# A list scheduler that takes a PSUM bank as one place, and another order of the three groups of a down turn

## The chip, the core and the metric

The kernel runs as one program on one core of one Trainium2 chip. The metric is device time in microseconds (us). Below, PE is TensorE, PEld its weight loads, DVE VectorE, ACT ScalarE, POOL GpSimd and SP the engine whose queue issues the DMAs.

## What is computed

A Performer attention (4 batches, 8 heads, 576 positions), then a mixture of 8 experts over all 2304 tokens, weighted by a Sinkhorn-normalised gate, then one dense layer with a swish. All in fp32.

```python
x = attention(q, k, v, omega)              # [2304, 512]
P = np.exp(x @ w_gate - max)               # [2304, 8]
for _ in range(8):
    P /= P.sum(1, keepdims=True) + 1e-09
    P /= P.sum(0, keepdims=True) + 1e-09
    P *= N / E
for e in range(E):
    out += P[:, e:e + 1] * (np.maximum(x @ w1[e], 0.0) @ w2[e])
h = out @ w_in
g = h * (1.0 / (1.0 + np.exp(-1.702 * h)))
return g @ w_out
```

## The kernel before

The attention comes first, with expert 0 woven into it (`e0_visit`, products on lines 716 and 773). Experts 1 to 7 and the dense layer follow in 54 **visits**, numbered 0 to 53 here: 18 pairs of 256-wide slices of the hidden layer (14 of experts, `l` = 0; 4 of the dense layer, `l` = 1) by 3 blocks of 768 tokens. A visit multiplies by Strassen's scheme (seven products in place of eight) in fp32 that is split into a high and a low part, three matmuls to a product term:

- `up_fast` makes the hidden layer: for each of the pair's two slices `c`, seven products of 6 matmuls (line 1152, 128x384): 84 matmuls in a visit. Their sums and differences are taken by ACT, DVE and POOL in banks 0 to 4 and 7 and in SBUF, and give the operands `h`.
- `down` multiplies `h` by the second weights: seven products `n` = 0 to 6, each in two **turns** (`c` = 0, then `c` = 1), each turn three **groups** `t` = 0, 1, 2 of 3 matmuls (line 1294, 128x256): 126 matmuls. The order of turns is written out in `TURNS`: (0,0), (0,1), (3,0), (1,0), (1,1), (2,0), (2,1), (3,1), (4,0), (4,1), (5,0), (5,1), (6,0), (6,1); the last one stands behind the first product of the next visit.

A PSUM bank holds two results of 256 columns. `PLACES` says where a group accumulates: "C" (n = 0, 2, 4, 6) in bank 5 (both halves, t = 0 and 1) and the first half of bank 6 (t = 2); "E" (n = 3, 5) in bank 7 (both halves) and the second half of bank 6; "D" (n = 1) in banks 0, 2 and 1. **So bank 6 belongs to C and to E.** After its turn c = 1 every group is evicted: by ACT into the banks of D for n = 0 (line 1311), otherwise onto the accumulator in SBUF by DVE (line 1329 for experts, line 1322 for the dense layer). A write to a bank waits in the running kernel until every earlier read of that bank is over, whichever half was read.

That order is made by `Plan`, a list scheduler that runs while the kernel is built. `rec` adds an operation with its engine, an assumed duration and the keys that it reads and writes. Operations that are `main` (all products of visits) stay on PE in the order written. `Plan.run` walks a modelled clock: each engine takes, when it is free, the arrived operation with the earliest due time; the resulting order is then issued. An operation marked "VP" may go to DVE or POOL. Before the change a bank's two halves are two keys (`spread` turns a whole bank into both), and a DVE or ACT operation occupies its engine for its whole duration. The Sinkhorn iterations (`sinkhorn`, lines 849 to 870, one small PE matmul each on line 862) are planned in the same way, among expert 0's last visits and visit 0. `y_operands` (transposes on line 955, sums on line 972) rebuilds operands at the change from experts to dense layer, in visits 40 to 43; `double_piece` (lines 1082 to 1106) converts the dense layer's weights, a few DVE operations a visit, during the experts.

Of the kernel before, what the change touches and what calls it, by code (L numbers as in the profile page):

```python
# [14 lines left out]
ALU = mybir.AluOpType  # L15
# [9 lines left out]
class Plan:  # L25
# [9 lines left out]
    AHEAD = 3.0  # L35

# [56 lines left out]
    def run(self):  # L93
# [12 lines left out]
        while done < len(self.ops):  # L106
# [66 lines left out]
def tile_performer_sinkhorn_moe(  # L173
# [437 lines left out]
    def spread(keys):  # L611

        return [h for k in keys for h in ([k + (0,), k + (1,)] if k[0] == "b" and len(k) == 2 else [k])]

    def rec(eng, dur, fn, r=(), w=(), **kw):
# [3 lines left out]
        else:  # L619
            plan.add(eng, dur, fn, spread(r), spread(w), **kw)  # L620
# [7 lines left out]
    def ps_us(n):  # L628
        return 0.17 + 0.001 * n
# [195 lines left out]
    def sinkhorn():  # L825
# [22 lines left out]
        for _ in range(NITER):  # L848
            dve(lambda: V.tensor_reduce(out=r[:, :, 0], in_=pg, op=ALU.add, axis=AX.X), ["lg"], ["r"])
            dve(lambda: V.tensor_scalar(out=r, in0=r, scalar1=1e-9, scalar2=None, op0=ALU.add), ["r"], ["r"], 0.12)  # L850
            dve(lambda: V.reciprocal(out=rr, in_=r), ["r"], ["rr"], 0.2)
            dve(
                lambda: V.tensor_tensor(out=pg, in0=pg, in1=rr.to_broadcast([P, NTILE, E]), op=ALU.mult),
                ["lg", "rr"], ["lg"],
# [3 lines left out]
                ["lg"], ["cs"],  # L858
# [9 lines left out]
            dve(lambda: V.reciprocal(out=rc[:, 0, :], in_=ct), ["ct"], ["rc"], 0.15)  # L868
# [5 lines left out]
                ["lg", "rc"], ["lg"],  # L874
# [406 lines left out]
    def down(l, e, j, first, final):  # L1281

        touched = set()
        for n, c in TURNS[l]:
# [3 lines left out]
            for t in range(3):  # L1288
# [3 lines left out]
                def fn(e, i=i, u=u, t=t, c=c, a=a, slot=slot, start=start, half=half):  # L1292
                    for m, (x, y) in enumerate(((0, 0), (0, 1), (1, 0))):
                        nc.tensor.matmul(  # L1294
                            bank[i][:, u], T["h", c, a, x][:, t * P : (t + 1) * P], T["w2", c, y][:, slot],
                            start=start and half == 0 and c == 0 and m == 0, stop=c == 1 and m == 2,
                            skip_group_check=True,
                        )

                wr = [("b", i, half)]  # L1300
                if start and half == 0 and c == 0:
                    wr = [("b", i)]
                rec("PE", 3 * 0.118, fn, down_reads(c, a, slot), wr, main=True)
                if c == 0:
                    continue
                rd = [("b", i, half)]
                if n == 0:
# [3 lines left out]
                        lambda e, i=i, d=d, u=u: nc.scalar.copy(bank[d][:, 0:FC], bank[i][:, u]),  # L1311
                        [("b", i, half)], [("b", d)],
# [213 lines left out]
```

## Time and profile before

| | us |
|---|---|
| median of 3 runs (lowest, highest) | 2136.28 (2135.95, 2139.05) |
| the profiled execution's own time | 2134.32 |
| its span, first to last instruction | 2132.6 |

In the profile a row of PE is a run of equal matmuls, with its start, its length and the number of instructions; in square brackets stands the idle time before it and what ended that. Matmuls overlap: the distance from one start to the next is the pace, not the duration of one.

### The profile page before, as it was taken

What the parts mean: (1) busy time and instruction counts of PE and PEld (TensorE: products, weight loads), DVE (VectorE), ACT (ScalarE), POOL (GpSimd) and SP (SyncE); (2) the same over time, 40 slices, a digit from 0 to 9 for tenths busy, and PEclk for the clock granted to TensorE, in tenths of its full rate; (3) what the DMA queues carried; (4) which work ended last, traced back from release to release, by engine and by line L of the source; (5) the groups of instructions that cost most, each with busy time, mean ns of one, the idle gap of its engine ahead of it and who ended that gap; (6) DMA issues with size and microseconds to landing.
All of it is one profiled execution on the core that took longest, in us unless ns stands there. A gap on an engine that the chain in (4) does not pass through costs nothing.

```text
span 2132.6 us, 38364 instructions
## 1 busy us (share of the span) xinstructions
PE 2054.1 (96%) x13938; PEld 1977.8 (93%) x13938; DVE 1484.8 (70%) x2962; ACT 1050.4 (49%) x2444; POOL 1149.9 (54%) x1086
## 2 busy tenths in 40 slices
PE   9999998799999999999999999999999989999998
PEld 8999987799999999999999999999999979999998
DVE  7666559867667766777766776777666776667766
ACT  7655544355444443544444354444435466745644
POOL 3112239548465764747666574756647364737442
PEclk9999999999999999999999999999999999999999
DMA  8333238747556655746665675566456797645543
GB/s 165 85 80 90 70 98 300 248 175 276 193 205 239 245 192 216 261 179 222 253 224 187 227 259 191 208 256 222 184 207 227 240 294 252 235 152 212 221 175 128
DMA packets 255948, 431.46 MB, mean 202 GB/s; under 512 B 73744, under 2 KB 197136, under 8 KB 255760
## 3 DMA queue, kind: packets, MB, share of 16 engines
q1 hardware_dynamic: 255760, 429.02, 57.9%
q8 instruction: 110, 1.80, 0.3%
q14 instruction: 78, 0.64, 0.1%
HBM read 382.81 MB, written 46.14 MB: 201 GB/s over the span
## 4 chain that ended last, share of the span: by engine, by line
PE 79%; DVE 14%; ACT 2%; issue 2%; DMA 2%; POOL 1%; SPq 0%; DVEq 0%; ACTq 0%; POOLq 0%
PE bank L1152 34%; PE bank L1294 31%; DVE acc L1329 6%; PE ph L716 3%; PE py L773 3%; PE num L431 2%; DVE ring L639 1%; DMA sx<-stage 1%; PE kv L401 1%; DVE acc L1322 1%; DVE h L639 1%; PE pt L342 1%; DVE bank L1173 1%; PE pj L367 1%; PE pj L368 1%
## 5 line engine op out<-in xcount | busy, mean ns | idle before, releaser
L1294 PE MATMUL bank<-w,h 128*128 128x256 f32 x6804 | 892.8, 286 | 47.9 <-DVE acc L1329 28.4
L1294 PEld LDWEIGHTS bank<-w,h 128*128 128x128 f32 x6804 | 848.4, 191 | 86.4 <-DVE acc L1329 49.7
L1152 PE MATMUL bank<-xo,w 128*128 128x384 f32 x4536 | 821.5, 336 | 2.8 <-ACT ring L1162 1.9
L1152 PEld LDWEIGHTS bank<-xo,w 128*128 128x128 f32 x4536 | 783.7, 189 | 5.8 <-ACT ring L1162 4.0
L639 POOL TENSOR_TENSOR w<-raw,w 128x768 fp32r<-128x768 f32 (+1 forms) x216 | 327.5, 1524 | 313.4 <-ACT w L1058 302.6
L1329 DVE SCALAR_TENSOR_TENSOR acc<-bank,lg,acc 128x256 f32<-128x256 f32 x756 | 319.5, 478 | 200.8 <-PE bank L1294 200.0
L639 POOL TENSOR_TENSOR h<-ring,h 128x384 fp32r<-128x384 f32 x321 | 348.5, 1107 | 133.9 <-ACT h L1162 130.1
L1162 ACT ACTIVATE ring<-bank 128x384 f32<-128x384 f32 x432 | 210.2, 491 | 132.5 <-PE bank L1152 125.9
L1162 ACT ACTIVATE bank<-bank 128x384 f32<-128x384 f32 x108 | 51.4, 476 | 442.1 <-PE bank L1152 419.1
L1162 ACT ACTIVATE h<-ring 128x384 fp32r<-128x384 f32 x432 | 207.1, 527 | 87.4 <-DVE ring L1184 63.2
L639 POOL TENSOR_TENSOR raw<-raw 128x256 f32<-128x256 f32 x283 | 212.0, 774 | 47.0 <-DMA raw<-in_moe_w_dram 27.5
L1211 DVE SCALAR_TENSOR_TENSOR h<-bank,h 128x384 fp32r<-128x384 f32 x252 | 137.2, 552 | 120.5 <-ACT ring L1162 103.5
L1162 ACT ACTIVATE h<-bank 128x384 fp32r<-128x384 f32 x324 | 157.6, 492 | 62.8 <-DVE bank L1173 34.9
L1184 DVE SCALAR_TENSOR_TENSOR ring<-bank,ring 128x384 f32<-128x384 f32 x336 | 172.4, 548 | 20.6 <-PE bank L1152 20.0
L1058 ACT CAST w<-raw 128x768 fp32r<-128x768 f32 (+1 forms) x216 | 146.6, 691 | 81.0 <-POOL raw L639 65.2
L639 POOL TENSOR_TENSOR ring<-ring,ring 128x384 f32<-128x384 f32 (+1 forms) x97 | 103.4, 1066 | 142.9 <-ACT ring L1162 139.8
L695 POOL TENSOR_TENSOR egl<-raw,egh 128x512 fp32r<-128x512 f32 x32 | 41.9, 1327 | 187.4 <-ACT egh L692 168.9
L1173 DVE TENSOR_TENSOR bank<-bank,ring 128x384 f32<-128x384 f32 x216 | 120.9, 561 | 30.4 <-PE bank L1152 27.9
L639 DVE TENSOR_TENSOR h<-ring,h 128x384 fp32r<-128x384 f32 x111 | 112.0, 1024 | 22.4 <-ACT h L1162 21.9
L387 ACT ACTIVATE feat<-pj,nb 128x128 f32<-128x128 f32 x272 | 74.2, 387 | 67.2 <-DVE nb L383 64.9
L1322 DVE TENSOR_TENSOR acc<-bank,acc 128x256 f32<-128x256 f32 x180 | 65.7, 418 | 40.4 <-PE bank L1294 40.0
L1173 DVE TENSOR_TENSOR bank<-bank,sig 128x384 f32<-128x384 f32 x96 | 53.5, 561 | 50.1 <-ACT sig L1162 48.8
(231 smaller groups left out, 2084.2 us busy)
## 6 DMA issues: line engine op xcount, KB each, us to landing
xo<-sx SPq DMA_DIRECT2D x378, 768.0 KB, 7.1
raw<-in_moe_w_dram SPq DMA_DIRECT2D x288, 128.0 KB, 4.4
sx<-stage SPq DMA_DIRECT2D x126, 128.0 KB, 4.2
sx<-ring SPq DMA_DIRECT2D x48, 192.0 KB, 2.6
raw<-in_moe_w_dram SPq DMA_DIRECT2D x16, 512.0 KB, 4.1
stage<-in_moe_w_in_dram SPq DMA_DIRECT2D x16, 512.0 KB, 8.0
stage<-in_moe_w_out_dram SPq DMA_DIRECT2D x16, 512.0 KB, 6.7
k<-in_k_dram SPq DMA_DIRECT2D x16, 256.0 KB, 4.1
```

The costliest lines, as they stand in the source:

```text
L387: nc.scalar.activation(f[:, h, :], pvs[h // 4][:, h % 4, :], AF.Exp, bias=nb[:, h : h + 1])
L639: lambda e: e.tensor_tensor(out=out(), in0=a(), in1=b(), op=op),
L716: nc.tensor.matmul(o, ws[a], xs[b], start=m == 0, stop=m == n - 1, skip_group_check=True)
L1058: lambda e, a=a, b=b: nc.scalar.copy(T[w, c, 0][:, a:b], r[:, a:b]), raws, [(w, c, g, 0)],
L1152: nc.tensor.matmul(o(b), T["w1", c, a][:, slot, kk], T["xo"][x][:, y, kk], start=start and kk == 0 and n == 0, stop=kk == 1 and n == 2, sk ...
L1162: rec("ACT", act_us(Q), lambda e: nc.scalar.activation(out(), src(), f, **kw), r, w)
L1173: lambda e: e.tensor_tensor(out=out[0](), in0=a[0](), in1=b[0](), op=op), [a[1], b[1]], [out[1]],
L1184: lambda e: e.scalar_tensor_tensor(out=RT(out), in0=o(b), scalar=0.0, in1=RT(c), op0=ALU.max, op1=op),
L1211: lambda e: e.scalar_tensor_tensor(out=g(), in0=src[0](), scalar=0.0, in1=h().bitcast(F32), op0=ALU.max, op1=ALU.subtract),
L1294: nc.tensor.matmul(bank[i][:, u], T["h", c, a, x][:, t * P : (t + 1) * P], T["w2", c, y][:, slot], start=start and half == 0 and c == 0 an ...
L1322: lambda e, q=q, i=i, u=u: e.tensor_tensor(out=q, in0=bank[i][:, u], in1=q, op=ALU.add),
L1329: lambda e, q=q, i=i, u=u, g=g: e.scalar_tensor_tensor(out=q, in0=bank[i][:, u], scalar=g, in1=q, op0=ALU.mult, op1=ALU.add),
```

## The change

Four things are changed in the planner and the order it is given, and none in what is computed:

1. A bank is one key: `spread` is gone, and an eviction reads, a group writes `("b", i)`.
2. In a turn c = 1 the groups are taken in the order t = 2, 0, 1, and for n = 3 in the order 0, 2, 1; in turns c = 0 as before. The evictions of a turn are recorded behind its third group, in the same order.
3. An engine other than PE is free again 0.07 us before its operation's end (`LEAP`), and a PE operation that had to wait is planned 0.1 us longer (`RESTART`).
4. Assumed durations: a down group 0.36 in place of 0.354, an eviction on line 1329 0.05 longer, and the Sinkhorn steps.

```diff
+    LEAP = 0.07
+    RESTART = 0.1
...
-                o = None
+                o, rest = None, 0.0
...
                         if t - at["PE"] > 0.02:
+                            rest = self.RESTART
...
-                    d = o.dur[e] if isinstance(o.dur, dict) else o.dur
-                    o.end = at[e] = t + d
+                    d = (o.dur[e] if isinstance(o.dur, dict) else o.dur) + rest
+                    o.end = t + d
+                    at[e] = o.end if e in ("PE", "X") else o.end - self.LEAP
...
-            plan.add(eng, dur, fn, spread(r), spread(w), **kw)
+            plan.add(eng, dur, fn, r, w, **kw)
...
-            dve(lambda: V.tensor_scalar(out=r, in0=r, scalar1=1e-9, scalar2=None, op0=ALU.add), ["r"], ["r"], 0.12)
+            dve(lambda: V.tensor_scalar(out=r, in0=r, scalar1=1e-9, scalar2=None, op0=ALU.add), ["r"], ["r"], 0.3)
...
-            for t in range(3):
+            order = (0, 1, 2) if c == 0 else (0, 2, 1) if n == 3 else (2, 0, 1)
+            for t in order:
...
-                def fn(e, i=i, u=u, t=t, c=c, a=a, slot=slot, start=start, half=half):
+                def fn(e, i=i, u=u, t=t, c=c, a=a, slot=slot, s=start and half == 0 and c == 0):
...
-                wr = [("b", i, half)]
-                if start and half == 0 and c == 0:
-                    wr = [("b", i)]
-                rec("PE", 3 * 0.118, fn, down_reads(c, a, slot), wr, main=True)
-                if c == 0:
-                    continue
-                rd = [("b", i, half)]
+                rec("PE", 3 * 0.12, fn, down_reads(c, a, slot), [("b", i)], main=True)
+            if c == 0:
+                continue
+            for t in order:
+                i, half = PLACES[b][t]
+                u = slice(half * FC, (half + 1) * FC)
+                rd = [("b", i)]
...
-                        "DVE", ps_us(FC),
+                        "DVE", ps_us(FC) + 0.05,
```

The other planned Sinkhorn durations go to 0.27 and 0.2 (the reciprocals, from 0.2 and 0.15), 0.98 (the row scaling, from 0.3), 0.43 (the column sum, from 0.3) and 0.7 (the column scaling, from 0.3).

On PE, in the turn n = 4, c = 1 of an expert visit (`h14..` is its operand; `bank5`, `bank6` the banks), before:

```order
L1294 MATMUL bank5_3771<-w210_4561,h140_4571 128x256
L1294 MATMUL bank5_3771<-w211_4562,h140_4571 128x256
L1294 MATMUL bank5_3771<-w210_4561,h141_4572 128x256
L1294 MATMUL bank5_3771<-w210_4561,h140_4571 128x256
L1294 MATMUL bank5_3771<-w211_4562,h140_4571 128x256
L1294 MATMUL bank5_3771<-w210_4561,h141_4572 128x256
L1294 MATMUL bank6_3772<-w210_4561,h140_4571 128x256
L1294 MATMUL bank6_3772<-w211_4562,h140_4571 128x256
L1294 MATMUL bank6_3772<-w210_4561,h141_4572 128x256
```

and now:

```order
L1295 MATMUL bank6_3772<-w210_4560,h140_4570 128x256
L1295 MATMUL bank6_3772<-w211_4561,h140_4570 128x256
L1295 MATMUL bank6_3772<-w210_4560,h141_4571 128x256
L1295 MATMUL bank5_3771<-w210_4560,h140_4570 128x256
L1295 MATMUL bank5_3771<-w211_4561,h140_4570 128x256
L1295 MATMUL bank5_3771<-w210_4560,h141_4571 128x256
L1295 MATMUL bank5_3771<-w210_4560,h140_4570 128x256
L1295 MATMUL bank5_3771<-w211_4561,h140_4570 128x256
L1295 MATMUL bank5_3771<-w210_4560,h141_4571 128x256
```

The group in bank 6 has moved from third place to first.

On DVE, the evictions of one expert visit from n = 1 (banks 0, 1, 2) to n = 5, before:

```order
L1329 SCALAR_TENSOR_TENSOR acc0_126<-bank0_3766,lg_77,acc0_126 128x256
L1329 SCALAR_TENSOR_TENSOR acc0_126<-bank2_3768,lg_77,acc0_126 128x256
L1329 SCALAR_TENSOR_TENSOR acc0_126<-bank1_3767,lg_77,acc0_126 128x256
L639 TENSOR_TENSOR h141_4572<-ring9_3793,h140_4571 128x384
L1329 SCALAR_TENSOR_TENSOR acc0_126<-bank5_3771,lg_77,acc0_126 128x256 x2
L1329 SCALAR_TENSOR_TENSOR acc0_126<-bank6_3772,lg_77,acc0_126 128x256
L1329 SCALAR_TENSOR_TENSOR acc0_126<-bank7_3773,lg_77,acc0_126 128x256 x2
L1329 SCALAR_TENSOR_TENSOR acc0_126<-bank6_3772,lg_77,acc0_126 128x256
L1329 SCALAR_TENSOR_TENSOR acc0_126<-bank5_3771,lg_77,acc0_126 128x256 x2
L1329 SCALAR_TENSOR_TENSOR acc0_126<-bank6_3772,lg_77,acc0_126 128x256
```

and now:

```order
L639 TENSOR_TENSOR h121_4567<-ring11_3795,h120_4566 128x384
L1328 SCALAR_TENSOR_TENSOR acc0_126<-bank1_3767,lg_77,acc0_126 128x256
L1328 SCALAR_TENSOR_TENSOR acc0_126<-bank0_3766,lg_77,acc0_126 128x256
L1328 SCALAR_TENSOR_TENSOR acc0_126<-bank2_3768,lg_77,acc0_126 128x256
L1328 SCALAR_TENSOR_TENSOR acc0_126<-bank6_3772,lg_77,acc0_126 128x256
L1328 SCALAR_TENSOR_TENSOR acc0_126<-bank5_3771,lg_77,acc0_126 128x256 x2
L1328 SCALAR_TENSOR_TENSOR acc0_126<-bank6_3772,lg_77,acc0_126 128x256
L1328 SCALAR_TENSOR_TENSOR acc0_126<-bank7_3773,lg_77,acc0_126 128x256 x2
L1328 SCALAR_TENSOR_TENSOR acc0_126<-bank6_3772,lg_77,acc0_126 128x256
L1328 SCALAR_TENSOR_TENSOR acc0_126<-bank5_3771,lg_77,acc0_126 128x256 x2
```

Bank 6 is now evicted ahead of the pair in bank 5 or 7 of the same turn, where it stood behind it.

On PE in visit 0, the sixth of the eight Sinkhorn matmuls (line 862) among the up products, before:

```order
L1152 MATMUL bank3_3769<-xo0_3777,w111_4179 128x384
L1152 MATMUL bank3_3769<-xo0_3777,w110_4178 128x384
L862 MATMUL bank7_3773<-sm_153,ones_72 128x8
L1152 MATMUL bank0_3766<-xo4_3781,w100_4176 128x384
L1152 MATMUL bank0_3766<-xo4_3781,w101_4177 128x384
```

and now:

```order
L1152 MATMUL bank1_3767<-xo5_3782,w101_4181 128x384
L1152 MATMUL bank1_3767<-xo5_3782,w100_4180 128x384
L862 MATMUL bank7_3773<-sm_153,ones_72 128x8
L1152 MATMUL bank4_3770<-xo1_3778,w110_4182 128x384
L1152 MATMUL bank4_3770<-xo1_3778,w111_4183 128x384
```

It stands two products (12 matmuls) later. The seventh and the eighth stand where they stood, next to each other behind the tenth product: five products after the sixth before, three now.

## Rows read from the trace of the kernel before

**Rows 1.** The page's head and PE's busy share (us, share, instructions).
```profile
span 2132.6 us, 38364 instructions
...
PE 2054.1 (96%) x13938; PEld 1977.8 (93%) x13938; DVE 1484.8 (70%) x2962; ACT 1050.4 (49%) x2444; POOL 1149.9 (54%) x1086
```

**Rows 2.** The page's chain that ended last: share by engine, then by line.
```profile
PE 79%; DVE 14%; ACT 2%; issue 2%; DMA 2%; POOL 1%; SPq 0%; DVEq 0%; ACTq 0%; POOLq 0%
```

**Rows 3.** Busy time by stretch: visits 1 to 39, 40 to 42, 43 to 52.
```profile
core 0: us, PE busy (x) PEld busy (x) DVE busy (x) ACT busy (x) POOL busy (x), PEclk, DMA share, GB/s
441.02:1661.79 1220.77, 1193.09 (x8193) 1165.07 (x8192) 847.89 (x1684) 546.16 (x1209) 744.50 (x691) 1.00 0.60 219
1661.79:1779.93 118.14, 103.62 (x705) 99.97 (x703) 89.46 (x198) 71.38 (x180) 57.77 (x56) 0.96 0.91 284
1779.93:2095.58 315.65, 308.69 (x2102) 299.45 (x2101) 214.53 (x444) 179.65 (x416) 165.24 (x156) 1.00 0.56 204
```

**Rows 4.** Timeline of PE, one visit without waits at its start: pace of both products.
```profile
724.84 12.65 PE L1152 MATMUL bank<-xo,w 128*128 128x384 f32 x72
737.33 1.23 PE L1294 MATMUL bank<-w,h 128*128 128x256 f32 x9
738.39 1.21 PE L1152 MATMUL bank<-xo,w 128*128 128x384 f32 x6
```

**Rows 5.** Timeline of PE, the end of visit 19: three waits.
```profile
1029.00 3.61 PE L1294 MATMUL bank<-w,h 128*128 128x256 f32 x27 [0.28 <-DVE acc L1329]
1032.89 2.42 PE L1294 MATMUL bank<-w,h 128*128 128x256 f32 x18 [0.28 <-DVE acc L1329]
1035.60 0.62 PE L1294 MATMUL bank<-w,h 128*128 128x256 f32 x3 [0.28 <-DVE acc L1329]
...
1037.10 1.23 PE L1294 MATMUL bank<-w,h 128*128 128x256 f32 x9
1038.17 2.07 PE L1152 MATMUL bank<-xo,w 128*128 128x384 f32 x11
```

**Rows 6.** Timeline of PEld, the second of these waits.
```profile
1032.89 2.21 PEld L1294 LDWEIGHTS bank<-w,h 128*128 128x128 f32 x18 [0.49 <-DVE acc L1329]
```

**Rows 7.** Timeline of DVE, the same stretch: evictions in threes.
```profile
1031.57 1.27 DVE L1329 SCALAR_TENSOR_TENSOR acc<-bank,lg,acc 128x256 f32<-128x256 f32 x3 [1.43 <-PE bank L1294]
1034.27 1.27 DVE L1329 SCALAR_TENSOR_TENSOR acc<-bank,lg,acc 128x256 f32<-128x256 f32 x3 [1.43 <-PE bank L1294]
...
1038.02 1.27 DVE L1329 SCALAR_TENSOR_TENSOR acc<-bank,lg,acc 128x256 f32<-128x256 f32 x3 [1.42 <-PE bank L1294]
```

**Rows 8.** Who waited for whom, whole kernel (us, times, longest).
```profile
DVE acc L1329 <- PE bank L1294: 200.0, 188, 2.5
...
PEld bank L1294 <- DVE acc L1329: 49.7, 105, 0.8
...
PEld bank L1294 <- DVE acc L1322: 8.0, 25, 0.7
```

**Rows 9.** Waits of PE alone in visits 1 to 39.
```profile
PE bank L1294 <- DVE acc L1329: 27.0, 97, 0.5
PE bank L1152 <- ACT ring L1162: 0.6, 3, 0.2
```

**Rows 10.** Groups by shape, whole kernel (busy us, mean ns, idle before).
```profile
L1329 DVE SCALAR_TENSOR_TENSOR acc<-bank,lg,acc 128x256 f32<-128x256 f32 x756 | 319.5, 478 | 200.8 <-PE bank L1294 200.0
...
L639 DVE TENSOR_TENSOR h<-ring,h 128x384 fp32r<-128x384 f32 x111 | 112.0, 1024 | 22.4 <-ACT h L1162 21.9
...
L1322 DVE TENSOR_TENSOR acc<-bank,acc 128x256 f32<-128x256 f32 x180 | 65.7, 418 | 40.4 <-PE bank L1294 40.0
...
L1311 ACT COPY bank<-bank 128x256 f32<-128x256 f32 x162 | 53.7, 365 | 47.0 <-PE bank L1294 44.3 <-DVE ring L1184 2.0
```

**Rows 11.** Timeline of DVE around visit 19: two steps of `double_piece`.
```profile
1035.46 0.42 DVE L1082 TENSOR_SCALAR stage<-stage 128x512 uint32<-128x512 uint32 x1
1035.91 0.69 DVE L1086 SCALAR_TENSOR_TENSOR stage<-stage 128x512 uint32<-128x512 uint32 x1
```

**Rows 12.** Timeline of PE in visit 0: the seventh and eighth Sinkhorn matmuls (two instructions each).
```profile
403.68 5.45 PE L1152 MATMUL bank<-xo,w 128*128 128x384 f32 x30
413.71 0.60 PE L862 MATMUL bank<-sm,ones 128*128 128x8 f32 x2 [4.58 <-DVE sm L857]
418.14 0.60 PE L862 MATMUL bank<-sm,ones 128*128 128x8 f32 x2 [3.84 <-DVE sm L857]
419.60 5.34 PE L1152 MATMUL bank<-xo,w 128*128 128x384 f32 x18 [0.86 <-DVE bank L1173]
```

**Rows 13.** Timeline of DVE there: operations between the Sinkhorn steps.
```profile
407.50 0.41 DVE L639 TENSOR_TENSOR raw<-raw 128x256 f32<-128x256 f32 x1
...
411.85 1.48 DVE L639 TENSOR_TENSOR raw<-raw 128x256 f32<-128x256 f32 x1
```

**Rows 14.** Timeline of PE in visits 41 and 42: the longest waits.
```profile
1719.82 1.43 PE L1294 MATMUL bank<-w,h 128*128 128x256 f32 x9 [4.20 <-DVE stage L972]
...
1762.13 2.29 PE L1294 MATMUL bank<-w,h 128*128 128x256 f32 x9 [6.62 <-DVE stage L972]
```

More of the change, by code (lines that the diff above doesn't have):

```diff
@@ L609, in tile_performer_sinkhorn_moe @@
     live = [True]
-    def spread(keys):
-        return [h for k in keys for h in ([k + (0,), k + (1,)] if k[0] == "b" and len(k) == 2 else [k])]
     def rec(eng, dur, fn, r=(), w=(), **kw):
@@ L849, in sinkhorn @@
             dve(lambda: V.tensor_reduce(out=r[:, :, 0], in_=pg, op=ALU.add, axis=AX.X), ["lg"], ["r"])
-            dve(lambda: V.tensor_scalar(out=r, in0=r, scalar1=1e-9, scalar2=None, op0=ALU.add), ["r"], ["r"], 0.12)
-            dve(lambda: V.reciprocal(out=rr, in_=r), ["r"], ["rr"], 0.2)
+            dve(lambda: V.tensor_scalar(out=r, in0=r, scalar1=1e-9, scalar2=None, op0=ALU.add), ["r"], ["r"], 0.3)
+            dve(lambda: V.reciprocal(out=rr, in_=r), ["r"], ["rr"], 0.27)
             dve(
                 lambda: V.tensor_tensor(out=pg, in0=pg, in1=rr.to_broadcast([P, NTILE, E]), op=ALU.mult),
-                ["lg", "rr"], ["lg"],
+                ["lg", "rr"], ["lg"], 0.98,
             )
@@ L857, in sinkhorn @@
                 lambda: V.tensor_reduce(out=cs, in_=pg.rearrange("p t e -> p e t"), op=ALU.add, axis=AX.X),
-                ["lg"], ["cs"],
+                ["lg"], ["cs"], 0.43,
             )
@@ L867, in sinkhorn @@
             )
-            dve(lambda: V.reciprocal(out=rc[:, 0, :], in_=ct), ["ct"], ["rc"], 0.15)
+            dve(lambda: V.reciprocal(out=rc[:, 0, :], in_=ct), ["ct"], ["rc"], 0.2)
             dve(
@@ L873, in sinkhorn @@
                 ),
-                ["lg", "rc"], ["lg"],
+                ["lg", "rc"], ["lg"], 0.7,
             )
@@ L1295, in fn @@
                             bank[i][:, u], T["h", c, a, x][:, t * P : (t + 1) * P], T["w2", c, y][:, slot],
-                            start=start and half == 0 and c == 0 and m == 0, stop=c == 1 and m == 2,
-                            skip_group_check=True,
-                        )
-                wr = [("b", i, half)]
-                if start and half == 0 and c == 0:
-                    wr = [("b", i)]
-                rec("PE", 3 * 0.118, fn, down_reads(c, a, slot), wr, main=True)
-                if c == 0:
-                    continue
-                rd = [("b", i, half)]
+                            start=s and m == 0, stop=c == 1 and m == 2, skip_group_check=True,
+                        )
+                rec("PE", 3 * 0.12, fn, down_reads(c, a, slot), [("b", i)], main=True)
[5 more added lines that the diff above has]
+                rd = [("b", i)]
                 if n == 0:
@@ L1310, in down @@
                         "ACT", act_us(FC),
-                        lambda e, i=i, d=d, u=u: nc.scalar.copy(bank[d][:, 0:FC], bank[i][:, u]),
-                        [("b", i, half)], [("b", d)],
+                        lambda e, i=i, d=d, u=u: nc.scalar.copy(bank[d][:, 0:FC], bank[i][:, u]), rd, [("b", d)],
                     )
```

## The prediction

> **What bounds the kernel now.** I read the page's head first: PE is busy 96% of the span [rows 1], and the chain that ended last is PE for 79% and DVE for 14% [rows 2]. So PE sets the time, and the question is what PE waits for in its own stream. The stretches tell where the span lies: visits 1 to 39 take 1220.8 us, visits 40 to 42 take 118.1, visits 43 to 52 take 315.7 [rows 3]. Everything else (attention, expert 0, visit 0, the last visit) issues much the same order as before.
>
> What would visits 1 to 39 cost without a wait? The pace of an up matmul is (737.33 - 724.84)/72 = 0.1735 us, that of a down matmul (738.39 - 737.33)/9 = 0.118 [rows 4], or (1038.17 - 1037.10)/9 = 0.119 [rows 5]. A visit is then 84 x 0.1735 + 126 x 0.119 = 29.6 us and 39 of them 1153; 68 us are lost, 1.7 a visit. The waits name the loser: DVE's eviction on line 1329 ends 97 waits of PE in these visits, ACT 3 [rows 9].
>
> The timeline shows one such wait closely. Three times at the end of visit 19 PE stops for an eviction, with 18 matmuls between two stops [rows 5]. The profile shows 0.28 us idle, but that isn't the price: weights are held too, for 0.49 us [rows 6], and from one stopped matmul to the next 18 matmuls take 1035.60 - 1032.89 = 2.71 us in place of 2.16 or a little less. **A stop costs 0.55 us**, and 97 of them are 53 of the 68 us.
>
> Why it stops: 18 matmuls are two turns, so the stop is at the same place of each turn pair, the third group (bank 6). DVE evicts in threes, 0.395 us from start to start ((1.27 - 0.48)/2), and starts the first of them at 1031.57 [rows 7], so the third starts at 1032.36 and ends at 1032.84; PE goes on at 1032.89 [rows 5]. That third eviction was bank 6's, behind the pair of bank 5 or 7. PE fills bank 6 as the third group of a turn, wants it again as the third group of the next, two groups later, and gets there first. That it waits although the other half is meant shows that a bank is one place in the running kernel.
>
> **The change, part by part.**
>
> *Bank 6 first, and evicted first.* I set a turn c = 1 at time 0, matmuls 0.119 apart. How long an eviction starts behind the last matmul of its group I read at visit 20's start: the sixth of nine matmuls begins at 1037.10 + 5 x 0.119 = 1037.70 [rows 5], the first eviction at 1038.02 [rows 7]; so 0.32 us. Bank 6's group now begins its last matmul at 0.24, its eviction runs 0.56 to 1.04, and PE may write at 1.09.
> - n = 2 to n = 3: the next write of bank 6 is the 13th matmul, at 1.43, its weights 0.12 earlier. 0.2 us to spare.
> - n = 3 to n = 4 (n = 3 evicts bank 6 as soon as DVE is through with n = 2, at 2.07; done at 2.6): wanted at 2.9. 0.3 to spare.
> - n = 4 to n = 5 and n = 5 to n = 6: wanted as the 16th matmul, at 1.79, its weights at 1.67. 0.6 to spare.
>
> So the stops at bank 6 go. In the whole kernel PE's weights waited 105 times, 49.7 us, for line 1329 and 25 times, 8.0 us, for line 1322 [rows 8]; with the 0.06 by which a stop costs more than its 0.49, that is 57.7 + 130 x 0.06 = 65.5 us. About 1.5 of it is in visits 40 to 42, where other waits follow: **64 us** off. Of the 68 - 53 = 15 us that the stops don't explain, some are waits too short to show, next to the stops; I count a third, **5 us**. The ends are 0 and 15.
>
> *What is late next.* The pair of bank 5 or 7 is now evicted behind its second group, which is the turn's last. For n = 2: last matmul at 0.95, evictions at 1.27 and 1.67, the second over at 2.14, PE free to write at 2.19. The turn (4,0) wants bank 5 as the 19th matmul, at 2.14, its weights at 2.02. **PE comes 0.17 us too early**, in every visit. The trace of before doesn't hold this wait; its ends are 0 (if 0.32 is a little long) and a full stop, 0.55. I take 0.17, worked out from the spacing: 40 visits x 0.17 = 6.8. For n = 3, 4 and 5 the pair has a turn more and is through in time. In 8 expert visits the new DVE order has a step of `double_piece` (0.42 or 0.69 us [rows 11]) ahead of one of n = 2's or n = 3's or n = 4's bank evictions; I charge 0.3 each (ends 0 and 0.7): 2.4. In two visits an eviction of n = 1 has come between bank 6 and bank 5: 2 x 0.4 = 0.8. In the 11 visits of the dense layer an eviction of n = 1 often comes there too; its duration is 0.418 [rows 10], the stop then some 0.25: 2.8. Together **12.8 us** back on.
>
> The Trainium skill (VectorE: DVE Perf Modes, The DRAIN you can't avoid) says that the next operation doesn't start until the engine's pipe is empty, though one that isn't held may. By the first half the second eviction would end 0.08 later and 51 visits would lose 4 us more; the spacing of 0.395 against 0.48 [rows 7] speaks for the overlap.
>
> *Copies of n = 0.* They are taken by ACT behind the turn's third group, 0.36 us later than before for t = 0; 0.365 each [rows 10]. Bank 0 is wanted a turn later (1.07 us), bank 2 a group after it: copies over at 1.27 + 0.37 = 1.64 and 2.0, against 2.02 and 2.38. Covered while ACT is free; it waited 44 us for PE before these copies [rows 10]. Ends 0 and 3, I take **1.5 us** lost.
>
> *Sinkhorn.* PE idles 4.58 + 3.84 + 0.86 us around the last two matmuls of line 862 [rows 12]. They stand behind the same ten products now, so PE gains only if DVE ends sooner. On DVE the order up to the last Sinkhorn step has two operations of line 639 fewer, 0.4 to 1.5 us each [rows 13]; but the sixth matmul is 12 x 0.1735 = 2.1 us later in PE's stream, and work that lay between the seventh and eighth steps lies before the seventh. **1.5 us** off, ends 8 off and 5 on.
>
> *Operands of the dense layer.* Visits 41 and 42 wait 4.20 and 6.62 us for line 972 [rows 14]. Two transposes of visit 41 have moved forward by two products, two of visit 42 are one product later or earlier. With DMA at 0.91 [rows 3] I can't tell what ends that wait: 0, ends 6 off and 6 on.
>
> *Other queues.* SP issues the same transfers, a visit every 30.2 us in place of 31.3; DMA is at 0.60 of its time in visits 1 to 39, DVE at 848/1221 = 69%, POOL at 61% [rows 3]. A 4% faster visit leaves all of them room, so I charge nothing; if that cover fails, the up products would wait, which they hardly do now (0.6 us [rows 9]).
>
> Sum: 64 + 5 - 12.8 - 1.5 + 1.5 = 56 us off. The profiled execution took 2134.3, so 2078.3; the median of the runs shown is 2.0 above it, so as a median **2080 us**.
>
> **The rivals.**
> - *Nothing takes the stops' place* (13%): the 0.17 doesn't bind and Sinkhorn and visits 41, 42 gain. For it: 0.17 is the difference of two larger numbers. Against: the order of DVE puts the pair last in every turn. 56 + 12.8 + 10 = 79 off: 2057, between 2048 and 2066.
> - *The stop moves to bank 5* (12%): the wait at (4,0) is a full 0.55, since something delays DVE a little. 51 x 0.38 = 19 less: 2099, between 2094 and 2112.
> - *Evictions one behind the other* (3%): 51 x 0.08 = 4 less: 2084.
> - *The change doesn't reach the stop* (3%): DVE's evictions would have to run in the old order. Against: in 21 visits the new order has the whole run bank 6, 5, 5, 6, 7, 7, 6, 5, 5, 6, 7, 7, 6, 5, 5 without a break, before in none. 2136.
> - *Slower* (3%): DVE, whose queue is in order, reaches n = 2's eviction of bank 6 late because planned durations moved an operand subtraction of 1.02 us [rows 10] ahead of it. It decides from (56 + 12.8)/51 = 1.35 us lost a visit, that is 1.6 us late with the 0.2 to spare: two such subtractions in every visit. Then 2140 to 2150. Against: line 1329 waited 200 us for PE [rows 8], not the reverse, and the subtractions stand ahead of n = 1's three evictions.
>
> **How the numbers follow.** My own case, 66%, lies between 2066 and 2094 by the ends above (short waits, copies, Sinkhorn, visits 41 and 42 partly cancel). The range 2060 to 2102 leaves out most of the first rival (9%), the upper end of the second (3%), the last two (6%): under 20%. About 0.2%, 4 us, is what a measurement here can tell. Faster 0.94, same 0.03, slower 0.03.
>
> **What would show it.** Right: in visits 1 to 39 PE's waits for the eviction line fall from 97 stops to few, none before the third group of (4,0), (5,0), (6,0) or of (3,1); the pace is 30.2 us a visit; a short wait stands at (4,0)'s first matmul with 18 matmuls since n = 2's last turn began. Wrong: stops of 0.28 us idle remain at that first matmul (second rival), or DVE shows evictions that begin later than 0.4 us behind their group (fifth), or up products wait for DMA, DVE or ACT, which now they hardly do.

## The result, and the profile after

| | median of runs (lowest, highest), us | ratio to before, 95% interval |
|---|---|---|
| before, on the same chip | 2137.66 (2135.95, 2142.86) | |
| after | 2089.08 (2087.20, 2089.87) | 0.9767 [0.9748, 0.9787] |

The change makes the kernel 48.6 us faster (2.3%). The forecast was 56 us off and 2080; 2089 lies in the range, on its slow side. The profiled execution took 2089.18 us, 45.1 less than the one before.

The head of the page after, its busy line and the chain by engine, against [rows 1, 2]:

```profile
span 2087.4 us, 38322 instructions
...
PE 2027.9 (97%) x13938; PEld 1974.3 (95%) x13938; DVE 1494.0 (72%) x2951; ACT 1049.5 (50%) x2444; POOL 1165.2 (56%) x1097
...
PE 81%; DVE 13%; ACT 2%; DMA 1%; issue 1%; POOL 0%; SPq 0%; DVEq 0%; ACTq 0%
```

PE is still the bound. Its busy time fell from 2054.1 to 2027.9 us with the same 13938 matmuls: of a stop's 0.55 us only 0.28 show as idle [rows 5], and the rest counts as busy, 97 x 0.27 = 26 us. Busy time by stretch, against [rows 3] (visits 1 to 39, 40 to 42, 43 to 52):

```profile
core 0: us, PE busy (x) PEld busy (x) DVE busy (x) ACT busy (x) POOL busy (x), PEclk, DMA share, GB/s
445.95:1625.36 1179.41, 1170.53 (x8192) 1159.14 (x8191) 864.31 (x1679) 546.88 (x1209) 753.84 (x692) 1.00 0.61 227
1625.36:1744.76 119.40, 103.52 (x704) 100.22 (x703) 91.85 (x200) 70.35 (x180) 56.30 (x55) 0.96 0.89 276
1744.76:2051.52 306.76, 302.67 (x2102) 298.29 (x2101) 205.92 (x439) 179.69 (x416) 171.93 (x165) 1.00 0.58 213
```

So 41.4 us come from visits 1 to 39 and 8.9 from visits 43 to 52; visits 40 to 42 lose 1.3, and what lies ahead of visit 1 **loses 4.9** (445.95 against 441.02); the rest gains 1.2.

PE's and then PEld's waits in visits 1 to 39. The first stood at 27.0 us and 97 times [rows 9]:

```profile
PE bank L1295 <- DVE acc L1328: 8.4, 16, 0.9
...
PEld bank L1295 <- DVE acc L1328: 11.8, 17, 1.1
...
PEld bank L1295 <- ACT bank L1311: 0.3, 1, 0.3
```

The 97 stops are gone, and 16 new, longer ones stand. The starts of the single matmuls show where. Before, the three stop places, ahead of the third groups of (3,1), (5,0) and (6,0), each cost 0.44 us at a stop, and 0.10 more between the stopped matmul and the next: 0.54 us together, the price of 0.55 that the prediction took. Bank 6's other third groups, in (3,0), (4,0), (4,1) and (5,1), lost another 10 us over the 39 visits in shorter waits. After, two places are left: 0.05 + 0.10 = 0.16 us at the first matmul of (4,0) in most visits (7.6 us over the 39, five longer ones of 0.33 to 1.02 us in visits 7, 8, 17, 28 and 29 included), and about 0.8 us ahead of bank 6's group in (3,1), in ten visits, 2, 5, 11 and so on, **all of them on the third token block** (9.1 us with what follows it). The sixteenth stop, 0.53 us, is ahead of (6,0)'s third group in visit 17. A visit on the third block takes 31.00 us in the mean, the others 29.86: 14.9 us over the 13, of which the stop at (3,1) is the largest part.

Visit 2 on PE, then DVE and POOL. The 57 matmuls are (0,1) to (2,1), six turns, and (3,1)'s first group; the stop is ahead of its second, bank 6:

```profile
492.77 6.99 PE L1295 MATMUL bank<-w,h 128*128 128x256 f32 x57
500.31 6.43 PE L1295 MATMUL bank<-w,h 128*128 128x256 f32 x51 [0.55 <-DVE acc L1328]
```
```profile
495.84 2.85 DVE L639 TENSOR_TENSOR h<-ring,h 128x384 fp32r<-128x384 f32 x2
498.61 3.63 DVE L1328 SCALAR_TENSOR_TENSOR acc<-bank,lg,acc 128x256 f32<-128x256 f32 x9
```
```profile
494.43 2.54 POOL L639 TENSOR_TENSOR w<-raw,w 128x512 fp32r<-128x512 f32 x2
```

Two operand subtractions stand ahead of the evictions, 1.4 us each (498.61 - 495.84 = 2.77 for two); n = 1's three evictions come next, and bank 6's is the fourth: 498.61 + 3 x 0.395 + 0.48 = 500.28, and PE goes on at 500.31. In visit 1 one subtraction of 1.01 us stands there, and PE doesn't wait:

```profile
465.50 1.01 DVE L639 TENSOR_TENSOR h<-ring,h 128x384 fp32r<-128x384 f32 x1
466.46 1.27 DVE L1328 SCALAR_TENSOR_TENSOR acc<-bank,lg,acc 128x256 f32<-128x256 f32 x3
```

This is the mechanism of the rival "slower", in ten of 39 visits and at 0.8 us, far from the 1.35 in every visit from which it would have decided.

The front, PE in visit 0, against [rows 12]:

```profile
408.80 0.28 PE L862 MATMUL bank<-sm,ones 128*128 128x8 f32 x2
408.93 3.37 PE L1152 MATMUL bank<-xo,w 128*128 128x384 f32 x18
418.27 0.59 PE L862 MATMUL bank<-sm,ones 128*128 128x8 f32 x2 [5.96 <-DVE sm L857]
423.20 0.59 PE L862 MATMUL bank<-sm,ones 128*128 128x8 f32 x2 [4.33 <-DVE sm L857]
424.65 6.13 PE L1152 MATMUL bank<-xo,w 128*128 128x384 f32 x18 [0.86 <-DVE bank L1173]
430.58 1.28 PE L1295 MATMUL bank<-w,h 128*128 128x256 f32 x9
```

The waits before the seventh and eighth Sinkhorn matmuls grew from 8.42 to 10.29 us.

Not all of the front's loss lies there. Up to 310 us PE issues the same matmuls, by their tiles, in the same order as before, yet at that place it is 1.9 us late. 1.3 us of this are 12 matmuls of line 716. They stand behind the same wait for DVE (1.00 us, before 0.99) and the same 16 small matmuls, but took 3.51 us at a granted clock of 0.58 in the mean, most of it at the lower level, 1.2 GHz; before they took 2.19 at 1.00, 2.4 GHz. After and then before (us, PE busy, PEld busy, PEclk, DMA share, GB/s):

```profile
290.14:293.65 3.51, 3.51 (x12) 3.20 (x12) 0.58 0.00 0
```
```profile
289.81:292.00 2.19, 2.19 (x12) 2.03 (x12) 1.00 0.00 0
```

### The profile page after: what moved, and what is told of

It is laid out like the page before. It is cut to its first block, busy times and chain, and to the rows that moved or that the text cites. A ratio compares the mean times of both kernels' runs of the same rounds, so it can differ in the third digit from the quotient of the medians.

```text
span 2087.4 us, 38322 instructions
## 1 busy us (share of the span) xinstructions
PE 2027.9 (97%) x13938; PEld 1974.3 (95%) x13938; DVE 1494.0 (72%) x2951; ACT 1049.5 (50%) x2444; POOL 1165.2 (56%) x1097
## 4 chain that ended last, share of the span: by engine, by line
PE 81%; DVE 13%; ACT 2%; DMA 1%; issue 1%; POOL 0%; SPq 0%; DVEq 0%; ACTq 0%
PE bank L1152 34%; PE bank L1295 33%; PE ph L716 3%; PE py L773 3%; DVE h L639 2%; DVE ring L1184 2%; PE num L435 2%; DVE acc L1328 2%; DVE ring L639 1%; PE kv L405 1%; DMA sx<-stage 1%; ACT h L1162 1%; DVE bank L1173 1%; PE bank L773 1%; DVE stage L972 1%
## 5 line engine op out<-in xcount | busy, mean ns | idle before, releaser
L1295 PE MATMUL bank<-w,h 128*128 128x256 f32 x6804 | 861.0, 284 | 25.5 <-DVE acc L1328 9.4
L1328 DVE SCALAR_TENSOR_TENSOR acc<-bank,lg,acc 128x256 f32<-128x256 f32 x756 | 328.2, 478 | 146.3 <-PE bank L1295 146.0
L639 POOL TENSOR_TENSOR h<-ring,h 128x384 fp32r<-128x384 f32 x341 | 371.3, 1113 | 91.9 <-ACT h L1162 90.3
L1184 DVE SCALAR_TENSOR_TENSOR ring<-bank,ring 128x384 f32<-128x384 f32 x336 | 167.9, 547 | 21.2 <-PE bank L1152 21.1
L639 POOL TENSOR_TENSOR ring<-ring,ring 128x384 f32<-128x384 f32 (+1 forms) x88 | 94.2, 1072 | 124.5 <-ACT ring L1162 121.2
L639 DVE TENSOR_TENSOR h<-ring,h 128x384 fp32r<-128x384 f32 x91 | 94.5, 1049 | 2.0 <-ACT h L1162 1.4
```

Source lines behind the costliest of these rows:

```text
L639: lambda e: e.tensor_tensor(out=out(), in0=a(), in1=b(), op=op),
L1184: lambda e: e.scalar_tensor_tensor(out=RT(out), in0=o(b), scalar=0.0, in1=RT(c), op0=ALU.max, op1=op),
L1295: nc.tensor.matmul(bank[i][:, u], T["h", c, a, x][:, t * P : (t + 1) * P], T["w2", c, y][:, slot], start=s and m == 0, stop=c == 1 and m = ...
L1328: lambda e, q=q, i=i, u=u, g=g: e.scalar_tensor_tensor(out=q, in0=bank[i][:, u], scalar=g, in1=q, op0=ALU.mult, op1=ALU.add),
```

## The experiments

A table first: spans of the profiled executions, cut at the same places (the stretch ahead of visit 1, three stretches of visits, and what follows visit 52; us), and each kernel's median and ratio to before.

| run | ahead of 1 | 1-39 | 40-42 | 43-52 | rest | median | ratio [95%] |
|---|---|---|---|---|---|---|---|
| before | 441.0 | 1220.8 | 118.1 | 315.7 | 37.0 | 2136.64 to 2137.66 | |
| after | 446.0 | 1179.4 | 119.4 | 306.8 | 35.9 | 2089.08 | 0.9767 [0.9748, 0.9787] |
| order alone (1) | 441.6 | 1204.3 | 127.7 | 318.2 | 37.3 | 2129.59 | 0.9962 [0.9949, 0.9975] |
| planner alone (2) | 445.1 | 1215.1 | 122.6 | 321.5 | 37.7 | 2144.98 | 1.0039 [1.0027, 1.0051] |
| old Sinkhorn durations (3) | 444.2 | 1181.3 | 116.2 | 306.6 | 36.2 | 2091.37 | 0.9782 [0.9769, 0.9794] |
| no LEAP, no RESTART (4) | 447.3 | 1167.8 | 122.7 | 307.7 | 36.3 | 2083.31 | 0.9749 [0.9737, 0.9762] |
| subtractions + 0.4 us (5) | 446.1 | 1172.7 | 117.6 | 307.8 | 37.0 | 2081.21 | 0.9745 [0.9731, 0.9758] |
| **key and order alone (6)** | 440.9 | 1167.4 | 119.9 | 305.8 | 37.4 | **2075.80** | 0.9716 [0.9703, 0.9729] |
| (4) with old Sinkhorn (7) | 443.2 | 1168.2 | 122.7 | 307.7 | 36.6 | 2079.01 | 0.9730 [0.9716, 0.9743] |
| no LEAP (8) | 446.2 | 1167.6 | 122.8 | 308.5 | 36.5 | 2084.26 | 0.9756 [0.9743, 0.9770] |
| order with due times (9) | 442.4 | 1192.7 | 122.8 | 309.5 | 37.5 | 2104.74 | 0.9849 [0.9835, 0.9862] |
| (6) with subtractions + 0.4 (10) | 446.9 | 1166.9 | 124.3 | 309.6 | 37.1 | 2083.46 | 0.9747 [0.9733, 0.9760] |

A row's spans are those of one execution. It is 5.1 us faster than the median for (3), 2.7 faster for (6) and 3.0 slower for (10). Also, up to 310 us PE issues the same matmuls in the same order in all twelve kernels, and yet it is late there, against before, by 1.9 us in after, 0.4 in (3), 2.3 in (4), 4.5 in (5), 1.7 in (7), 1.9 in (10) and under 0.1 in (6). One profile of each can't tell whether the kernel or the execution decides this **lag**; below it is taken off where two first columns are compared. The ratios' intervals of (4), (5) and (8) overlap with that of after, though none of their executions was as slow as the fastest of after (2087.20).

The first theory (mine): the order of the groups takes the stops away, and the planner's part only matters in that it must not undo it. Its rival: the planner's one-bank key does it.

**1. The order alone.** Part 2 of the change in the kernel before, with its half-bank keys, its planner and its durations.

```diff
-            for t in range(3):
+            order = (0, 1, 2) if c == 0 else (0, 2, 1) if n == 3 else (2, 0, 1)
+            for t in order:
...
-                if c == 0:
-                    continue
+            if c == 0:
+                continue
+            for t in order:
...
```

> The kernel before with the new order of groups in a turn and of the evictions behind it, and nothing else: halves are still separate keys, no LEAP, no RESTART, old durations. Theory 1 (the order of the groups alone takes the stops away): about 2090 us, no stop at bank 6. Theory 2 (the scheduler must know that a bank is one place, otherwise DVE's queue undoes the order): in DVE's order of this kernel the eviction of bank 6 of n = 3 stands behind the pair of bank 7 in most expert visits; the pair waits for the turn's third group, so bank 6 comes free at 1.27 + 2 x 0.395 + 0.48 + 0.05 = 2.6 us after the turn began and is wanted, weights first, at 1.67: a stop of some 0.9 us before the third group of (4,0), the other stops gone. 1.65 - 0.9 = 0.75 us saved in some 45 visits: about 2103, between 2095 and 2115.

Measured: 2129.59, a gain of 7 us: visits 1 to 39 gain 16.5, visits 40 to 42 lose 9.6. Both theories missed. The stops moved to other groups of bank 6. PE in visit 6, where they stand ahead of (3,0)'s third group (15 matmuls behind the start of (0,1)) and of (4,1)'s first (72 behind it):

```profile
614.08 7.24 PE L1295 MATMUL bank<-w,h 128*128 128x256 f32 x57 [0.28 <-ACT bank L1315]
...
622.00 4.54 PE L1295 MATMUL bank<-w,h 128*128 128x256 f32 x36 [0.67 <-DVE acc L1333]
```

Its DVE order, here from visit 1 with `bank_3772` as bank 6, `bank_3771` as bank 5 and `bank_3773` as bank 7, shows one way to such a stop. For n = 3 bank 7 is evicted twice and then bank 6, since with half keys nothing presses for bank 6's second half until n = 5, while the running kernel wants it free for (4,0):

```
L1333 SCALAR_TENSOR_TENSOR acc_126<-bank_3772,lg,acc_126 128x256
L1333 SCALAR_TENSOR_TENSOR acc_126<-bank_3771,lg,acc_126 128x256 x2
L1333 SCALAR_TENSOR_TENSOR acc_126<-bank_3773,lg,acc_126 128x256 x2
L1333 SCALAR_TENSOR_TENSOR acc_126<-bank_3772,lg,acc_126 128x256 x2
```

The trace agrees: visit 1's stop at (4,0)'s third group ends at 467.92, behind the third eviction of that turn (467.39 to 467.87). For the stops at (4,1) and (5,1) I have only a reading: half keys also let (4,0)'s write go out ahead of that eviction, which then waits for it, and the next turn's write waits for the eviction.

**2. The planner alone.** Everything but the order of the groups.

```diff
-            order = (0, 1, 2) if c == 0 else (0, 2, 1) if n == 3 else (2, 0, 1)
+            order = (0, 1, 2)
```

> The changed kernel with the groups of every turn in the old order 0, 1, 2; one key for a bank, LEAP, RESTART and the new durations stay. Theory 1 (order of the groups): the stops at bank 6 stay at 0.55 us, the time goes back to about 2130. Theory 2 (the scheduler's knowledge of the bank): in DVE's order of this kernel bank 6 is now evicted second of three, between the two of bank 5 or 7, in n = 2, 4 and 5; it comes free at 0.92 + 0.395 + 0.48 + 0.05 = 1.84 us and is wanted, weights first, at 1.67, so the stops fall from 0.55 to 0.17 us: 2095 to 2105.

Measured: 2144.98, 8 us slower than before, though visits 1 to 39 gain 5.7. The stops at (3,1), (5,0) and (6,0) fall to 0.16 us in most visits, as the second theory has it, but (4,0)'s third group now costs 0.36 + 0.10 us in 33 visits, and (3,1)'s up to 1.6 in 13. My reading is that the planner knows of the stops and can't avoid them, since with bank 6's group third in its turn its eviction can't start earlier. Visit 1 of this kernel, ahead of (4,0)'s third group:

```profile
470.79 5.25 PE L1295 MATMUL bank<-w,h 128*128 128x256 f32 x39 [0.20 <-DVE acc L1328]
```

So each half alone gives nearly nothing (-7, +8), and the two together 48 or more. That fits neither theory as I stated it; I read it so that the order makes room on PE, and the key makes DVE and ACT use it. The +8 isn't the key's alone: this run has `LEAP`, `RESTART` and the new durations too, and the key without them on the old order wasn't run.

**3. Old Sinkhorn durations** in the changed kernel (0.12, 0.2, 0.3, 0.3, 0.15, 0.3 in place of the new six).

> The changed kernel with the old planned durations of the Sinkhorn steps. Theory: the changed kernel loses some 5 us up to the end of visit 0 (start of visit 1 at 446.0 us in place of 441.0), and the new, longer Sinkhorn durations cause it, since they move the Sinkhorn matmuls apart among PE's products; without them the start of visit 1 is at 441 or earlier and the time about 2084. Rival: one key for a bank and LEAP cause it, since they also change the order of DVE there; then the start of visit 1 stays at 446 or comes later, and the time is 2089 or more. In this kernel all eight Sinkhorn matmuls stand ahead of visit 0's first product.

Measured: 2091.37, the same as after within the intervals, against the theory. Visit 1 starts 1.7 us earlier than after (444.24 against 445.95), but 1.5 of that is lag, and visits 1 to 39 are 1.9 longer. So in this kernel the Sinkhorn durations explain next to nothing of the front's 4.9 us.

**4. Without LEAP and RESTART.**

```diff
-    LEAP = 0.07
-    RESTART = 0.1
+    LEAP = 0.0
+    RESTART = 0.0
```

> The changed kernel with LEAP and RESTART at 0: an eviction is planned at 0.48 us and the next one behind its end, where the trace shows 0.395 from start to start. Theory: both are fine tuning, 2087 to 2093, with stops of under 1 us a visit as in the changed kernel. Rival: a DVE that is planned too slow puts evictions of n = 1 between those of n = 2 and gives more operand work to POOL; then visits with stops of 1 us come more often than every third, 2098 or more.

Measured: 2083.31, 6 us faster than after, against both theories. Visits 1 to 39 gain 11.6 us and visits 40 to 42 and the front lose 4.6. In visit 2, where PE stopped, DVE's order now has n = 2's bank 6 **ahead of** n = 1's evictions.

The second theory, from here: what is lost on the third token block comes from two subtractions that the planner takes for 1.0 us and that last 1.4; rival: from LEAP on the evictions.

**5. Subtractions planned 0.4 us longer** on DVE, in the changed kernel.

```diff
+        d = both_us(n)
+        if n == Q:
+            d["DVE"] += 0.4
...
-            both_us(n) if eng == "VP" else both_us(n)[eng],
+            d if eng == "VP" else d[eng],
```

> The changed kernel, with DVE's 128x384 operand subtractions (line 639) planned 0.4 us longer, at the 1.4 us that they take in the trace of the changed kernel beside POOL's own subtractions. Theory 1: what is still lost in every third visit (1 us more than in the two before, 13 times in visits 1 to 39) comes from such subtractions that the planner puts ahead of n = 2's eviction of bank 6 because it thinks them 1.0 us long. They go elsewhere, the third visits come down from 30.8 to 29.9 us, and the time is 2089 - 12 = 2077 (2074 to 2082). Theory 2: the order of DVE is set by LEAP on the evictions, not by the subtraction's duration: the third visits stay at 30.8 and the time at 2089 (2086 to 2092).

Measured: 2081.21. The time lies in the first theory's range, its account doesn't hold: visits 1 to 39 gain 6.7 us, not 12, and the third visits come down to 30.5, not 29.9. Visit 2 has no stop any more, but not as I expected: two subtractions still stand there, and the evictions begin no earlier.

```profile
497.91 0.91 DVE L642 TENSOR_TENSOR h<-ring,h 128x384 fp32r<-128x384 f32 x1
499.15 4.01 DVE L1331 SCALAR_TENSOR_TENSOR acc<-bank,lg,acc 128x256 f32<-128x256 f32 x10 [0.34 <-PE bank L1298]
```

They begin 499.15 - 476.20 = 22.95 us into the visit (after: 498.61 - 475.77 = 22.84), but the first of them is bank 6's, and n = 1's follow. So in visit 2 the stop needs two things: late DVE and n = 1's three evictions ahead of bank 6's. Either a true duration or the absence of LEAP takes the second away.

**6. Key and order alone.** The changed kernel without LEAP, RESTART and any of the new durations.

> The changed kernel with the one-bank key and the new order of groups alone: no LEAP, no RESTART, all planned durations as before. Theory 1: key and order together carry the whole gain, the rest of the change costs: visits 1 to 39 at 1168 to 1175, start of visit 1 back at 441 to 443, time 2075 to 2083. Theory 2: the planned durations of the down group and the eviction (0.36, +0.05) are needed, or else evictions come late again: visits 1 to 39 above 1180, time 2088 to 2105.

Measured: 2075.80, the fastest; the first theory's numbers. PE's waits in visits 1 to 39, and a visit's 108 down matmuls in one piece:

```profile
PE bank L1295 <- DVE acc L1328: 0.7, 3, 0.4
```
```profile
547.31 13.26 PE L1295 MATMUL bank<-w,h 128*128 128x256 f32 x108
560.41 1.21 PE L1152 MATMUL bank<-xo,w 128*128 128x384 f32 x6
```

Visits 1 to 39 take 1220.8 - 1167.4 = **53.4 us** less than before. That this is what 97 stops at 0.55 cost is chance: the stops' 53 us are gone and so are the 10 us of short waits at bank 6, but 8.2 us now stand at (4,0)'s first matmul and 1.6 at (3,1). Visit 1 starts where it did before.

**7. Without LEAP and RESTART, old Sinkhorn durations.** What is left beyond (6) is 0.36 for a down group and 0.05 more for an eviction.

> The changed kernel without LEAP and RESTART and with the planned Sinkhorn durations of before; the new durations of the down group and the eviction stay. Theory 1: the two repairs add: 2083 without LEAP and RESTART, 2 off for the front, and the 5 that visits 40 to 42 and the front had lost with them come back in part: 2078 (2075 to 2082). Theory 2: the front's loss is not the durations but any disturbed order there: 2083 (2082 to 2087).

Measured: 2079.01, the first theory's time. Against (4), visit 1 starts 4.1 us earlier, 3.5 without the lag: without LEAP the Sinkhorn durations do cost in the front. Against (6) it starts 2.3 later, but 1.7 of that is lag, so of the other two durations the front shows next to nothing. Visits 40 to 42 didn't come back.

**8. Without LEAP, with RESTART.**

> The changed kernel without LEAP, with RESTART. Theory 1: LEAP is what lets a DVE subtraction slip ahead of an eviction: the third visits lose no more than the others (29.9), visits 1 to 39 at 1168, time 2083 (2080 to 2086), as without both. Theory 2: RESTART, which plans PE later after every wait it foresees, is the one: the third visits stay at 30.8, time 2089 (2087 to 2092).

Measured: 2084.26, the first theory: as (4) within the intervals, visits 1 to 39 at 1167.6. LEAP is what costs there, 11.8 us; RESTART nothing that these runs can tell.

**9. Order alone, with due times for bank 6's evictions.** To see whether the key does more than set due times:

```diff
+                due = None
+                if i == 6 and n in (0, 2, 3, 4, 5):
+                    due = plan.clock + (0.354 if n == 2 else 0.708) - 0.17 - (act_us(FC) if n == 0 else ps_us(FC))
...
```

> The order of groups alone, with the two halves of a bank still two keys (as in the run that changed the order only), but with a due time for every eviction of bank 6 that the bank's next group, whichever its half, needs. Theory 1: the one key does nothing but set these due times; with them the stops that the order alone left (about 1 us a visit) go, visits 1 to 39 take 1167 to 1176 and the time is 2076 to 2088. Theory 2: the key also makes the planner's TensorE wait as the real one does, so that everything else is placed against a true clock; due times alone give little, visits 1 to 39 stay above 1190 and the time above 2105.

Measured: 2104.74, by its numbers the second theory, at its edge, though due times give 25 of the 54 us that lie between (1) and (6). Visits 1 to 39 come down from 1204.3 to 1192.7 where the key reaches 1167.4; visits 40 to 52 give 13.6 us more. What is left there:

```profile
PE bank L1295 <- DVE acc L1336: 4.9, 7, 0.8
PE bank L1295 <- DVE h L639: 4.0, 7, 0.6
PE bank L1152 <- ACT ring L1162: 3.3, 8, 0.9
```

In many visits n = 3's evictions now run in the order bank 7, 6, 7 where (6) has 6, 7, 7; my reading is that with half keys the first half of bank 7 is ready for eviction a group earlier, and DVE takes it. Waits for operands and ring sums also stand here that (6) lacks. So due times are a part of what the key does, not all; how the rest divides between readiness and the planner's clock wasn't tried.

**10. Key and order, subtractions planned 0.4 us longer.**

> One-bank key and new order alone (the fastest so far, 2075.8), with DVE's 128x384 operand subtractions planned 0.4 us longer. Theory 1: the true duration still helps where subtractions come ahead of evictions or at the change to the dense layer: 2070 to 2074. Theory 2: without LEAP no subtraction slips ahead of bank 6 any more, and nothing is left to win: 2075.8 within 3.

Measured: 2083.46, slower than (6) by 7.7, against both theories. In visits 1 to 39 it changed 0.5 us, as theory 2 has it. The profiled executions lie 13.4 us apart, more than the medians: the front lost 6.0, of which 1.8 is lag, visits 40 to 42 4.4 and visits 43 to 52 3.8. A planned duration acts wherever that operation stands; which waits grew in those three stretches wasn't followed. (5) carries the same edit.

## Why the prediction was right

**The bound, the stop and its price: right.** PE's stops at bank 6 were the loss, a stop cost 0.54 to 0.55 us, and with key and order alone all but a few of them are gone from visits 1 to 39. The 5 us for waits too short to show (ends 0 and 15) were too few by half: 10 us stood at bank 6's other third groups.

**Bank 6 gone as a stop: right at (4,0) and (5,0), at (6,0) in all visits but one, and at (3,1) in 29 visits of 39.** The step "n = 2 to n = 3: 0.2 us to spare" assumed that DVE is free when bank 6's last matmul is done. On the third token block it isn't, and the spare was the smallest that it gave. (For n = 3 to n = 4 it took the matmul at 2.9 and not its weights, 0.12 earlier; the spare there is 0.14 and not 0.3, and it was enough.) The prediction had the place and the mechanism (the rival "slower") and gave it no price in its own sum: 9.1 us in visits 1 to 39 were missing there. It argued that subtractions stand ahead of n = 1's evictions, as if that made them harmless; n = 1's evictions stand ahead of bank 6's, so both delay it.

**What is late next: right.** (4,0)'s first matmul was to come 0.17 us early in every visit, 6.8 us in all; the trace has 0.16 in most visits and 7.6 us over visits 1 to 39. The wait did bind (first rival). A stop of 0.33 to 1.02 us stands there in five visits; the second rival wanted 0.55 in every one.

**Evictions overlap: right.** Nine in visit 2 take 3.63 us, (3.63 - 0.48)/8 = 0.394 from start to start, as before. By the Trainium skill (VectorE: DVE Perf Modes, The DRAIN you can't avoid) an operation waits until the pipe is empty unless nothing holds it; the trace agrees with the second half.

**Copies of n = 0: not seen.** In visits 1 to 39 no wait of PE for them shows, and one of the weights, 0.3 us; the 1.5 us weren't lost there.

**Sinkhorn: wrong in sign.** The step was "1.5 us off, ends 8 off and 5 on", because the sixth matmul is 2.1 us later in PE's stream and DVE's order had two operations of line 639 fewer. It came out at +4.9 for all ahead of visit 1, 3.1 without the lag of 1.9 at 310 us, although visit 0's stops were gone (its down matmuls and last up product take 445.95 - 430.58 = 15.4 us against 441.02 - 424.77 = 16.2). In visit 0, from the sixth to the eighth matmul DVE needs 423.20 - 408.80 = 14.4 us, before 418.14 - 403.54 = 14.6: as long as before, so that the 2.1 us by which the sixth comes later are lost in full. The steps between, which would have had to shrink, ran beside POOL's subtractions and took longer: line 850 took 1.63 and 0.78 us there, before 0.17 twice. It runs eight times in the kernel, after and then before (minimum, median and maximum in ns):

```profile
L850 DVE TENSOR_SCALAR sm<-sm x8: 159/884/1851, 324.9 to 420.0; 128x18 f32<-128x18 f32 x8
```
```profile
L850 DVE TENSOR_SCALAR sm<-sm x8: 165/176/695, 336.6 to 416.6; 128x18 f32<-128x18 f32 x8
```

Further, PE ran the 18 matmuls behind the eighth in 430.58 - 424.65 = 5.93 us, before in 424.77 - 419.60 = 5.17: after the longer wait it ran them all at the lower level, 1.2 GHz (granted clock 0.50, first row), before only most of them (0.59, second row):

```profile
424.65:430.58 5.93, 5.93 (x19) 5.93 (x20) 4.19 (x9) 4.90 (x10) 3.41 (x6) 0.50 0.61 160
```
```profile
419.60:424.77 5.17, 5.17 (x18) 5.17 (x19) 3.61 (x7) 3.50 (x7) 3.10 (x3) 0.59 0.17 51
```

Visit 0 starts 3.2 us late (401.49, before 398.31): 1.9 us of this are the lag, the rest comes in expert 0's last visits. There the granted clock was 0.50 from 379.46 to 382.88, behind a wait of PE for DVE of 1.84 us, where before that wait took 1.11 and the clock stayed at 1.00. Without the lag, run 3 against after and run 7 against 4 put 0.2 and 3.5 us on the planned Sinkhorn durations; which step there is late stays open.

**Visits 41 and 42: right,** charged at 0, 1.3 us lost in visits 40 to 42.

In sum: 9.1 us on the third token block and some 6 in the front were missing. That the forecast was still only 11 us off in the profiled execution is in part luck: the short waits gave 5 us more than counted, and some small charges weren't needed. So is the pace of 30.2 us a visit that it named as a sign of being right: 1179.4/39 = 30.24, but as the mean of 29.86 and 31.00.

## What to carry to other kernels

A dependency key that is finer than the one the hardware program enforces lets a list scheduler press the wrong operation, and an order that makes room is worth little until the scheduler knows why the room is needed; test such a pair together, since here the order alone gained 7 us, the planner's part alone lost 8, and key and order together gained 61. When a planned duration comes from a trace, ask what ran beside it: one figure for an operation that takes 0.17 or 1.6 us moves work in places nobody looked at, and here the change was 13 us faster without its new durations, LEAP and RESTART than with them. When you count the time to spare at a place, count every operation that stands ahead on that queue, in each kind of visit.

## What the runs showed that I had not expected

DVE operations between SBUF tiles took very different times within one kernel. The one on line 850 has 128x18 elements and took between 0.16 and 1.85 us (rows above). One of its long runs stands where POOL ran three subtractions in a row:

```profile
412.86 1.63 DVE L850 TENSOR_SCALAR sm<-sm 128x18 f32<-128x18 f32 x1
```
```profile
412.65 4.96 POOL L639 TENSOR_TENSOR w<-raw,w 128x768 fp32r<-128x768 f32 x3 [0.26 <-ACT w L1058]
```

The operand subtraction varied threefold in visits 1 to 39 of the kernel after; the eviction, which reads PSUM, hardly varied in the whole kernel:

```profile
L639 DVE TENSOR_TENSOR h<-ring,h x63: 543/1064/1650, 465.5 to 1615.2; 128x384 fp32r<-128x384 f32 x63
...
L1328 DVE SCALAR_TENSOR_TENSOR acc<-bank,lg,acc x756: 466/477/487, 437.8 to 1706.5; 128x256 f32<-128x256 f32 x189
```

The long run of line 850 is about as long as one of POOL's three, 4.96/3 = 1.65 us. The Trainium skill (SBUF — State Buffer, SBUF: two separate sides) says that DVE and POOL share a pair of SBUF ports under an exclusive lock, which a DVE operation takes in a two-port mode or with two SBUF inputs (then only against a POOL operation that reads SBUF), and that the later of the two waits for the other's whole instruction. These rows agree: subtraction and step are held for up to a POOL operation, the eviction, with one large input in SBUF, isn't.

The single operations show it closely. Of the 63 subtractions, 60 start while a POOL operation runs, 0.2 to 1.3 us ahead of its end, and each ends 0.41 to 0.42 us behind that end, whatever its own start; the other three, with POOL idle or at its operation's end, take 0.54 to 0.55 us. Seven of line 850's eight runs end 0.03 us behind POOL's end; the eighth, with POOL idle, takes 0.16. So the time of such an operation is what is left of POOL's operation and a constant, which one planned figure can't hold. No run took POOL's work away.
